# A two-stage attention kernel: scores and q@kv as row halves, fp32r turns of x, a power on GpSimd for the norms, and a written order of work

## The chip, the cores and the metric

The kernel runs on one core of a Trainium2 chip. A core has five engines with queues of their own: TensorE (PE; its weight loads are listed apart as PEld), VectorE (DVE), ScalarE (ACT), GpSimd (POOL) and SyncE (SP), which here only issues DMAs. Each takes its instructions in the order in which the program wrote them, and waits on semaphores. TensorE's products land in PSUM, eight banks of 512 fp32 values on 128 partitions; everything else lives in SBUF. The metric is the device time of one execution in microseconds (us), as a median over runs.

## The reference

Two layers in a row, on 8 batches of 576 tokens. The first is linear attention with 8 heads of 64 and an RMS norm for each head and token:

```python
kv = np.einsum('bhsd,bhse->bhde', k, v)
out = np.einsum('bhsd,bhde->bhse', q, kv)
rms = np.sqrt(np.mean(out * out, axis=-1, keepdims=True) + 1e-06)
x = out / rms * g_norm            # then heads side by side: 512 features
```

The second is a mixture of four causal attention experts with a head of 64; each token uses the two experts with the highest gate logits:

```python
logits = x @ w_gate               # top 2 of 4, softmax over the two
q, k, v = x @ wq[e], x @ wk[e], x @ wv[e]
a = softmax(causal(scale * (q @ k.T)))
out += w[e] * (a @ v @ wo[e])     # for the token's two experts
```

## The kernel before

Tokens are cut into five blocks, four of 128 and a last one of 64. The kernel writes its work as named tasks, one or a few instructions each: `("out", b, i)` is q@kv of block i in batch b. `graph` (line 48) lists all tasks with an engine, a cost and what they need; `plan` (line 270) puts them in one order: it follows the engines on a model of their time, and among the tasks that can start within 0.025 us on the engine that is free first it takes the one with the lowest `urgency` (line 257), a due time from a table per kind of task, batch and index. `SWAP` (line 28) says which PSUM copies go to the other one of ScalarE and VectorE. The order is written out under a manual schedule, so each engine's queue holds its share of that one list, and tasks of neighbouring batches are interleaved in it.

The stages of a batch, with their lines:

- Loads. k and v of a batch come in two DMAs each (four in batch 0) and a remainder for the last 64 tokens; q of batches 0 and 1 comes in token blocks of [tokens, 512] and is turned by TensorE transposes (`q`, line 625; copy `qc`); q of the others comes in eight DMAs, as 32-token pieces, and is turned by VectorE. In batch 0 half of the loads are issued on ScalarE's queue, and behind them the norm's and gate's weights (`lg0`, line 552, eight DMAs). Projection weights come as `lw` and are multiplied by g_norm (`ws`, line 582, four on GpSimd and two on VectorE).
- `kv` (line 599): k^T v of two heads at once, as column halves of 64: one head's result lies on PSUM partitions 0 to 63, the other's on 64 to 127. `kvx` (line 612) copies it into a block-diagonal matrix of two heads, with zeros elsewhere, `kvc` (line 618) copies it once more, compactly; `kt`, `ktc`, `kg`, `kgc` (lines 638 to 665) turn that, multiply it by the gate weights and put the products beside kv, so that q@kv gives gate logits with it.
- `out` (line 667): q@kv, for each block four fp32 products of 128 rows and 136 columns (two heads of 64 and 4). `oc` copies it to o_sb, `sq` squares it on ScalarE, `red` sums on VectorE.
- `nw` (line 699): the inverse square root of all five blocks at once, as a bit trick and three Newton steps in eleven small VectorE operations. `gl`, `lg`, `m8`, `sh`, `ex`, `mk`, `gt`, `den`, `rd`, `gate` make the gates from it, all on VectorE but the exponential. `xm` (line 747) multiplies o_sb by it on GpSimd into x_tok; `x` (line 758) turns x_tok by four fp32 transposes a block, and `xc` copies it to xT as fp32r.
- `v`, `qp`, `kp` (lines 808 to 835) are the projections, for two experts at once (p = 0, 1). `kpc` (line 841) copies k in two halves, one for each expert, into tiles whose other 64 rows stay zero.
- `sc` (line 853): scores of two experts and one piece of keys. Each product contracts 128 rows, of which the zeros of kT blot out the other expert's. Four pieces j hold 2, 4, 4 and 2 products, of 512; 64 and 448; 320 and 192; and 64 columns. `exp` on ScalarE, the causal cut `msk` on GpSimd.
- `pv`, `rc`, `iv`, `oc2` weigh v by the scores and scale by gate and sum; `ot`, `otc` turn it; `y` (line 945) multiplies by wo, `yc` copies, `st` stores.

PSUM is split into three tiles of two banks ("bg": out, projections, scores, pv) and two of one bank ("sm": the rest), taken in turn.

Of the kernel before, what the change touches and what calls it, by code (L numbers as in the profile page):

```python
# [10 lines left out]
FP32 = mybir.dt.float32  # L11
FP32R = mybir.dt.float32r
BF16 = mybir.dt.bfloat16
I32 = mybir.dt.int32
# [3 lines left out]
NB, NCH, EP = 5, 4, 2  # L18
QPE = 2
# [3 lines left out]

LOADS = ("lk", "lv", "lkr", "lvr", "lq", "lg0", "lw", "lwo", "st")

SWAP = {
    "ws": (('q', 0), ('v', 0),), "qc": ((0, 4), (1, 0), (1, 1), (1, 3),),
    "oc": ((0, 0), (0, 1), (1, 2), (1, 3), (1, 4), (6, 1), (6, 2), (6, 3), (7, 2), (7, 3),),  # L30
    "xc": ((0, 0), (0, 1), (1, 0), (1, 2), (1, 4), (6, 0), (6, 2), (6, 3), (7, 2), (7, 4),),
    "vc": ((0, 0), (6, 0), (6, 1), (6, 2),), "qpc": ((0, 0), (1, 0), (7, 0), (7, 1),),
    "kpc": ((0, 0), (6, 0), (7, 0),), "otc": ((0, 1), (1, 0), (1, 1), (6, 0), (6, 1),),
    "yc": ((0, 1), (0, 4), (1, 0), (1, 1), (1, 2), (1, 3), (1, 4), (6, 2), (6, 3),), "kvx": ((1,), (6,), (7,),),
    "kvc": ((1,),), "ktc": ((7,),),
}


def swapped(n):
    return n[1:] in SWAP.get(n[0], ())  # L40


def earlier(n, m):

    return len(n) > 1 and isinstance(n[1], int) and n[1] < m[1]


def graph(B):
    t = {}

    def add(name, eng, hold, lat, needs=(), tiles=()):
        t[name] = (eng, hold, lat, [n for n in needs if n in t], list(tiles))

    def pe(name, hold, needs, tiles=()):
        add(name, "PE", hold, hold + 0.27, needs, tiles)

    def act(name, took, needs, tiles=()):
        add(name, "ACT", took - 0.10, took + 0.06, needs, tiles)

    def dve(name, took, needs, tiles=()):  # L60
        add(name, "DVE", took - 0.05, took + 0.05, needs, tiles)

    def pool(name, took, needs, tiles=()):
        add(name, "POOL", took - 0.03, took + 0.10, needs, tiles)

    def copy(name, on_act, on_dve, needs, tiles=(), first=dve):

        ways = ((dve, on_dve), (act, on_act))
        if first is act:
            ways = ways[::-1]  # L70
        make, took = ways[swapped(name)]
        make(name, took, needs, tiles)

    R5, R4, R2 = range(NB), range(NCH), range(EP)
    for b in range(B):

        q2 = "ACT" if b == 0 else "SP"
        for p in R4 if b == 0 else R2:
            lat = 0.92 if b == 0 else 1.84
            add(("lk", b, p), "SP", 0.55, lat, (), (("k", b),))  # L80
            add(("lv", b, p), q2, 0.55, lat, (), (("v", b),))
        add(("lkr", b), "SP", 0.65, 0.67, [("kv", b - 2, c) for c in R4])
        add(("lvr", b), q2, 0.65, 0.67, [("kv", b - 2, c) for c in R4])
        for i in R5 if b < QPE else range(8):
            lat = (1.32 if i < NF else 0.66) if b < QPE else 1.06
            add(("lq", b, i), q2 if i % 2 else "SP", 0.6, lat, (), (("q", b),))
        if b == 0:
            add(("lg0",), "ACT", LG0, 0.3)
            dve(("wg",), 0.85, [("lg0",)])
            for nm in "qkv":  # L90
                for p in R2:
                    add(("lw", nm, p), "SP", 0.55, 0.92, (), (("x", nm, p),))
                    name, nd = ("ws", nm, p), [("lw", nm, p), ("lg0",)]
                    (dve if swapped(name) else pool)(name, 0.60 if swapped(name) else 1.08, nd, (("x", nm, p),))
# [912 lines left out]
```

The softmax here doesn't subtract the row's maximum and nothing guards it: scores larger than these inputs give would overflow.

## Time and profile before

| what | value |
|---|---|
| median of 3 runs (lowest to highest) | 252.12 us (252.02 to 252.76) |
| profiled execution: span from first to last instruction | 250.9 us |
| profiled execution: own time | not listed apart; the median lies 1.2 us above its span |
| busy: PE, PEld, DVE, ACT, POOL | 221.2, 199.0, 180.0, 148.8, 81.1 us |
| mean granted TensorE clock | 0.977 |

The profile page gives each engine's busy time, the span in 40 slices in tenths, the chain of work that ended last, and groups of instructions: line, engine, operation, output<-inputs, shape and count, then busy time in us and mean of one in ns, then the engine's idle time just before them with what ended it. A matmul's record lasts from its start to a modelled end, and records of a stream overlap; so a group's mean is no price, and the distance between records is.

### The profile page before, as it was taken

Reading aid. Unit: us, or ns where it says so; the run is one execution under the profiler, and the core shown is the slowest. Engines: PE = TensorE matmul, PEld = TensorE weight load, DVE = VectorE, ACT = ScalarE, POOL = GpSimd, SP = SyncE. Lnnn points to the kernel's source line nnn. Section 1 sums busy time; section 2 is a strip of 40 time slices with the busy share of each in tenths; the row PEclk is TensorE's granted clock in tenths of the full one; section 3 lists DMA queues with packets and bytes.
Section 4 is the critical chain, followed back from the end, with each engine's and each line's share of the span. In section 5 each row is a group of like instructions: output and inputs, shape, how many; then the busy total and the mean of one; then the engine's idle time right before and its main releaser. Section 6 shows DMA issues by size and latency. Waiting matters only on the chain.

```text
span 250.9 us, 6366 instructions
## 1 busy us (share of the span) xinstructions
PE 221.2 (88%) x2456; PEld 199.0 (79%) x2456; DVE 180.0 (72%) x510; ACT 148.8 (59%) x258; POOL 81.1 (32%) x159
## 2 busy tenths in 40 slices
PE   0726957999999999999999998989999699999982
PEld 0714847999999879996998988979988699888850
DVE  0084698688898978998699928976878887794560
ACT  0003450664923976359738993488899556838973
POOL 8300016604800256006700920066006600902310
PEclk9999995999999999999999999999999899999998
DMA  6997999999999989895999993021034100104245
GB/s 172 302 163 223 288 243 283 231 135 285 189 161 332 136 165 343 120 240 184 247 129 272 220 167 103 3 86 42 3 123 173 42 0 3 43 3 146 79 156 189
DMA packets 99433, 40.28 MB, mean 161 GB/s; under 512 B 76618, under 2 KB 94538, under 8 KB 99402
## 3 DMA queue, kind: packets, MB, share of 16 engines
q1 hardware_dynamic: 94320, 38.15, 65.8%
q10 hardware_dynamic: 5082, 1.72, 3.2%
q8 instruction: 19, 0.31, 0.6%
q14 instruction: 12, 0.10, 0.2%
HBM read 30.43 MB, written 9.44 MB: 159 GB/s over the span
## 4 chain that ended last, share of the span: by engine, by line
PE 71%; DVE 11%; DMA 7%; ACT 7%; issue 1%; SPq 1%; ACTq 0%; DVEq 0%
PE p_out L670 13%; PE p_sc L858 9%; PE p_v L811 8%; PE p_k L829 7%; PE p_q L829 7%; PE p_kv L607 6%; PE p_x L625 6%; PE p_y L948 6%; PE p_pv L892 6%; DMA q_b<-in_q_dram 3%; ACT PT L872 3%; DMA k_b<-in_k_dram 3%; DVE sh L776 2%; PE p_q L625 2%; PE p_ot L936 1%
## 5 line engine op out<-in xcount | busy, mean ns | idle before, releaser
L878 POOL TENSOR_SCALAR_AFFINE_SELECT PT<-PT 128x256 bf16<-128x256 bf16 (+1 forms) x80 | 29.0, 383 | 102.0 <-ACT PT L872 87.0
L751 POOL TENSOR_TENSOR x_tok<-o_sb,rs 128x512 f32<-128x512 f32 (+1 forms) x40 | 41.6, 1121 | 54.0 <-DVE rs L725 51.5
L872 ACT ACTIVATE PT<-p_sc 128x128 bf16<-128x128 f32 (+1 forms) x64 | 51.4, 849 | 6.9 <-PE p_sc L858 6.5
L670 PE MATMUL p_out<-kvx,qT 128*128 128x136 f32 x320 | 44.8, 290 | 0.7 <-DVE kvx L493 0.5
L670 PEld LDWEIGHTS p_out<-kvx,qT 128*128 128x128 f32 x320 | 41.9, 199 | 1.4 <-DVE kvx L493 0.5
L858 PE MATMUL p_sc<-qTp,kT 128*128 128x64 f32 (+4 forms) x192 | 39.8, 335 | 0.6 <-ACT PT L872 0.4
L690 ACT ACTIVATE sq<-o_sb 128x512 f32<-128x512 f32 (+1 forms) x40 | 25.3, 637 | 19.2 <-DVE o_sb L493 16.8
L858 PEld LDWEIGHTS p_sc<-qTp,kT 128*128 128x128 f32 x192 | 28.5, 190 | 4.4 <-ACT PT L872 1.1
L696 DVE TENSOR_REDUCE ms<-sq 128x8 f32<-128x520 f32 (+1 forms) x40 | 27.2, 682 | 5.8 <-ACT sq L690 5.5
L493 DVE COPY o_sb<-p_out 128x544 f32<-128x544 f32 (+1 forms) x30 | 21.6, 719 | 13.3 <-PE p_out L670 12.8
L607 PE MATMUL p_kv<-v_b,k_b 128*64 128x64 f32 x512 | 21.7, 236 | 7.6 <-DMA k_b<-in_k_dram 7.5
L811 PE MATMUL p_v<-wv_r,xT 128*128 128x256 f32 x160 | 26.6, 296 | 0.9 <-DVE vext L493 0.7
L625 PE MATMUL p_x<-ident_f,x_tok 128*128 128x128 f32 (+1 forms) x160 | 23.4, 279 | 3.9 <-DVE mk L785 2.2
L607 PEld LDWEIGHTS p_kv<-v_b,k_b 128*64 128x64 f32 x512 | 19.3, 148 | 9.4 <-DMA v_b<-in_v_dram 7.3
L948 PE MATMUL p_y<-wo_b,OT 128*128 128x512 bf16 x80 | 22.7, 381 | 1.0 <-ACT xT L491 0.7
L811 PEld LDWEIGHTS p_v<-wv_r,xT 128*128 128x128 f32 x160 | 21.6, 189 | 2.2 <-DVE vext L493 1.0
L625 PEld LDWEIGHTS p_x<-ident_f,x_tok 128*128 128x128 f32 (+1 forms) x160 | 17.9, 146 | 6.2 <-issue 3.2
L491 ACT CAST xT<-p_x 128x512 fp32r<-128x512 f32 (+1 forms) x30 | 15.7, 546 | 10.6 <-PE p_x L625 10.5
L829 PE MATMUL p_k<-xT,wk_r 128*128 128x288 f32 x128 | 20.2, 301 | 0.0
L491 ACT COPY y<-p_y 128x512 f32<-128x512 f32 (+1 forms) x31 | 17.8, 593 | 3.8 <-PE p_y L948 2.6
L829 PE MATMUL p_q<-xT,wq_r 128*128 128x288 f32 x128 | 19.1, 299 | 0.0
L491 ACT CAST kT<-p_k 64x576 fp32r<-64x576 f32 x26 | 16.5, 634 | 4.2 <-PE p_k L829 4.0
(89 smaller groups left out, 325.1 us busy)
## 6 DMA issues: line engine op xcount, KB each, us to landing
out_dram<-y SPq DMA_DIRECT2D x32, 256.0 KB, 2.2
k_b<-in_k_dram SPq DMA_DIRECT2D x14, 512.0 KB, 5.5
v_b<-in_v_dram SPq DMA_DIRECT2D x14, 512.0 KB, 7.1
q_b<-in_q_dram SPq DMA_DIRECT2D x48, 144.0 KB, 4.8
q_b<-in_q_dram SPq DMA_DIRECT2D x6, 256.0 KB, 8.2
k_rem<-in_k_dram SPq DMA_DIRECT2D x8, 128.0 KB, 3.9
v_b<-in_v_dram ACTq DMA_DIRECT2D x4, 256.0 KB, 6.5
k_b<-in_k_dram SPq DMA_DIRECT2D x4, 256.0 KB, 6.3
```

Source lines behind the costliest of these rows:

```text
L491: nc.scalar.copy(dst, src)
L607: nc.tensor.matmul(p_kv[hh * Dh : (hh + 1) * Dh, c, :], lhsT=lhs, rhs=rhs, start=(j == 0), stop=(j == NF), skip_group_check=True,)
L625: nc.tensor.transpose(p_t[:, c, :nt], chunk(c)[:nt], ident_f[:nt, :nt])
L670: nc.tensor.matmul(p_o[:, c // 2, (c % 2) * 256 : (c % 2) * 256 + 2 * GW], lhsT=blocks_of(qT, c)[:, i * P : (i + 1) * P], rhs=kvx[b % 2][: ...
L696: nc.vector.tensor_reduce(mss[b % 2][:nt, i, :], sqs[(NB * b + i) % 3][:nt], axis=AX_X, op=AluOpType.add)
L751: nc.gpsimd.tensor_tensor(out=buf(("x", b, i), [P, NCH, P], FP32, "x_tok")[:nt].rearrange("p c (h r) -> p h r c", h=H), in0=ob[:nt, i, :, ...
L811: nc.tensor.matmul(p_v[:], lhsT=blocks_of(xTs[b % 2], c)[:, i * P : (i + 1) * P], rhs=w_r["v"][:, c, :, :].rearrange("p e f -> p (e f)"), ...
L829: nc.tensor.matmul(p_p[:, s, 0:HALF], lhsT=w_r[nm][:, c, 2 * pr : 2 * pr + 2, :].rearrange("p e f -> p (e f)"), rhs=blocks_of(xTs[b % 2], ...
L858: nc.tensor.matmul(p_s[:, el, o : o + hi - lo], lhsT=kTs[pr][el][:, kb * P : (kb + 1) * P], rhs=tiles["qTp", b, pr][:, lo:hi], start=True, ...
L872: nc.scalar.activation(PT[:, :, d0 : d0 + o], big("sc", b, pr, j)[:, :, 0:o], ACTF.Exp, scale=scale)
L878: nc.gpsimd.affine_select(out=d, in_=d, compare_op=AluOpType.is_ge, fill=0.0, base=0, pattern=[[0, 2], [1, w]], channel_multiplier=-1,)
L948: nc.tensor.matmul(p_y[:], lhsT=blocks_of(OTs[b % 2], pr)[:, qc * P : (qc + 1) * P], rhs=wo_b[:, pr, :], start=(pr == 0), stop=(pr == EP - 1),
```

## The change

Each part in the words of the code:

- **Scores.** kT is one tile of 128 rows with both experts' keys (three of them in turn), copied by one instruction. A product takes one expert's 64 rows of kT and of qT; the two experts' products go to different PSUM banks.
- **q@kv.** kvx is compact: for each pair of heads, the heads' kv side by side with their gate columns at the outer ends. A block takes eight products of 64 rows and 68 columns, alternating between the lower and the upper 64 rows, into two banks. The copies `kvx` and `kvc` become one, and `kt` reads kvx.
- **Head pairs.** Heads c and c + 4 are always paired, in all batches; so q of batches 0 and 1 is loaded in two DMAs for each block (it was one), and the gate weights for the other pairing go (two DMAs fewer in `lg0`).
- **Gates of kv (`kg`).** Four products with an output of 64 columns of the array each, two for each half, in place of two full ones; one copy.
- **Norms.** The mean's factor 1/64 goes into g_norm (`g8` multiplies by 8). `pw` raises a block's sums to the power -0.5 on GpSimd, one operation of 128x8 for each block; Newton is gone. 18 of 40 squares are done on GpSimd by a multiplication. Of the small gate operations, 7 of 8 `sh`, 3 of 8 each of `gl`, `gt` and `gate`, and 19 of 32 `iv` are on GpSimd.
- **x.** Its turn is an fp32r product with an identity, in all blocks with 128 rows.
- **Last y block.** 64 tokens by 512 columns become two column halves, on partitions 0 to 63 and 64 to 127; the copy is 128x256, the store two DMAs.
- **Order, engines and buffers.** `graph`, `plan` and the tables go. The order of all tasks, the engine of each, and the slot of each buffer stand in three strings; PSUM is four pairs of banks, in which a task takes a pair or one bank as the string says. Moved with it: 25 of 40 o_sb copies on ScalarE (10 before), 14 of 40 xT copies (30 before), 20 of 40 vext copies (4 before), all weight products on VectorE.

```diff
-    kTs = []
-    for pr in range(EP):
-        pair = []
-        for el in range(2):
-            t = const.tile([P, NB, P], FP32R, name=f"kT{pr}{el}")
...
     def k_proj_copy(b, pr):
-        for el in range(2):
-            pb = slice(el * Hd, (el + 1) * Hd)
-            copy(
-                ("kpc", b, pr), kTs[pr][el][pb, 0:S].rearrange("p (s n) -> p s n", s=2), big("k", b, pr)[pb, :, 0:HALF]
-            )
+        t = kTs[(2 * b + pr) % 3]
+        copy(("kpc", b, pr), t[:, 0:S].rearrange("p (s n) -> p s n", s=2), big("k", b, pr)[:, :, 0:HALF])
...
         for kb, lo, hi in PIECES[j]:
             for el in range(2):
+                pp = slice(el * Hd, (el + 1) * Hd)
                 nc.tensor.matmul(
                     p_s[:, el, o : o + hi - lo],
-                    lhsT=kTs[pr][el][:, kb * P : (kb + 1) * P],
-                    rhs=tiles["qTp", b, pr][:, lo:hi],
+                    lhsT=kTs[(2 * b + pr) % 3][pp, kb * P : (kb + 1) * P],
+                    rhs=tiles["qTp", b, pr][pp, lo:hi],
...
-    def kvx_copy(b):
-        p_kv = small(None, "kv", b)[:, 0]
-        for hh in range(2):
-            pp = slice(hh * Dh, (hh + 1) * Dh)
-            copy(("kvx", b), kvx[b % 2][pp, :, hh, 0:Dh], p_kv[pp, :, :])
+    def kv_copy(b):
+        copy(
+            ("kvc", b), kvx[b % 2][:, :, E : E + 2 * Dh],
+            small("kv", b)[:, 0 : NCH * Dh].rearrange("p (m f) -> p m f", m=EP),
+        )
...
         for c in range(NCH):
-            nc.tensor.matmul(
-                p_o[:, c // 2, (c % 2) * 256 : (c % 2) * 256 + 2 * GW],
-                lhsT=blocks_of(qT, c)[:, i * P : (i + 1) * P],
-                rhs=kvx[b % 2][:, c, :, :].rearrange("p a g -> p (a g)"),
+            for hh in range(2):
+                pp = slice(hh * Dh, (hh + 1) * Dh)
+                nc.tensor.matmul(
+                    p_o[:, hh, c * GW : (c + 1) * GW],
+                    lhsT=blocks_of(qTs[b % NQT], c)[pp, i * P : (i + 1) * P],
+                    rhs=kvx[b % 2][pp, c // 2, c % 2 * GW : (c % 2 + 1) * GW],
...
+    def pw(b, i):
+        nc.gpsimd.tensor_tensor(
+            out=rstds[b % 2][:, i * H : (i + 1) * H], in0=mss[b % 2][:, i, :],
+            in1=minus_half[:].to_broadcast([P, H]), op=AluOpType.pow,
+        )
...
     def x_tr(b, i):
-        transpose_in(i, lambda c: tiles["x", b, i][:, c, :], "x", b, i)
+        p_t, nt = small("x", b, i), blocks[i][1]
+        for c in range(NCH):
+            nc.tensor.matmul(
+                p_t[:, c * P : c * P + nt], lhsT=tiles["x", b, i][:, c, :], rhs=ident_r[:, 0:nt], start=True, stop=True
+            )
...
     def sh(b):
-        nc.vector.tensor_tensor(
+        ew(("sh", b)).tensor_tensor(
...
     def y_mm(b, qc):
-        p_y = small([P, D], "y", b, qc)
+        p_y, (s0, nq) = small("y", b, qc), blocks[qc]
         for pr in range(EP):
-            nc.tensor.matmul(
-                p_y[:], lhsT=blocks_of(OTs[b % 2], pr)[:, qc * P : (qc + 1) * P], rhs=wo_b[:, pr, :],
-                start=(pr == 0), stop=(pr == EP - 1),
-            )
+            lhs = OTs[b % 2][:, pr * S + s0 : pr * S + s0 + nq]
+            for o in range(P // nq):
+                w = D * nq // P
+                nc.tensor.matmul(
+                    p_y[o * nq : (o + 1) * nq, 0:w], lhsT=lhs, rhs=wo_b[:, pr, o * w : (o + 1) * w],
+                    start=(pr == 0), stop=(pr == EP - 1), skip_group_check=True,
+                )
...
+    psum = ctx.enter_context(tc.tile_pool(name="ps", bufs=1, space=bass.MemoryType.PSUM))
+    pairs = [psum.tile([P, 2, 512], FP32, name=f"p_{j}") for j in range(4)]
+    def small(*key):
+        n = place(("sm",) + key)
+        return pairs[n // 2][:, n % 2, :]
...
     with tc.manual_schedule():
-        for t, _, n in plan(tasks, POOLS, {n: urgency(n) for n in tasks})[0]:
+        for n in order:
             emit[n[0]](*n[1:])
```

## The prediction

> **What bounds the kernel now.** I read the page's span, busy times and slices first, then the busy time by stage, the groups of instructions, and last the chain of waits, for prices.
>
> ```profile
> span 250.9 us, 6366 instructions
> ...
> PE 221.2 (88%) x2456; PEld 199.0 (79%) x2456; DVE 180.0 (72%) x510; ACT 148.8 (59%) x258; POOL 81.1 (32%) x159
> ...
> PE   0726957999999999999999998989999699999982
> ...
> PEclk9999995999999999999999999999999899999998
> ```
>
> The reader sees TensorE full from the seventh slice to the end. By stage (columns: PE, PEld, DVE, ACT, POOL, clock, DMA share, GB/s):
>
> ```profile
> 0.00:60.00 60.00, 40.65 (x436) 36.79 (x438) 35.25 (x93) 17.29 (x32) 16.84 (x45) 0.94 1.00 227
> 60.00:150.00 90.00, 89.13 (x1080) 82.09 (x1077) 74.47 (x217) 61.19 (x107) 34.29 (x59) 1.00 1.03 212
> 150.00:240.00 90.00, 85.92 (x899) 77.51 (x898) 67.35 (x190) 64.87 (x109) 29.59 (x55) 0.98 0.19 63
> 240.00:251.00 11.00, 5.46 (x54) 2.58 (x51) 2.96 (x12) 5.49 (x11) 0.41 (x1) 0.93 0.50 180
> ```
>
> TensorE idles 19.4 us in the first 60, 0.9 in the next 90, 4.1 in the third stage and 5.5 at the tail: 29.8 us of 250.9. Only TensorE work, the start and those gaps can pay. The costliest TensorE groups:
>
> ```profile
> L670 PE MATMUL p_out<-kvx,qT 128*128 128x136 f32 x320 | 44.8, 290 | 0.7 <-DVE kvx L493 0.5
> ...
> L858 PE MATMUL p_sc<-qTp,kT 128*128 128x64 f32 (+4 forms) x192 | 39.8, 335 | 0.6 <-ACT PT L872 0.4
> ```
>
> Their busy times hold pipeline tails, so prices come from pieces of the chain of waits (start, us, what):
>
> ```profile
> 55.51 1.31 PE p_kv L607 x40
> ...
> 101.42 0.47 PE p_v L811 x4
> ...
> 109.41 2.48 PE p_kv L607 x80
> 111.89 0.68 PE p_v L811 x4
> ...
> 121.19 0.93 PE p_out L670 x8
> ...
> 234.80 0.47 PE p_sc L858 x2
> ...
> 236.15 1.37 PE p_sc L858 x10
> ```
>
> A q@kv block costs 0.93 us: eight records (each fp32 product shows as two), 0.116 apart. One head pair's twelve score products cost 0.47 + 1.37 = 1.84. The kv records are 2.48/80 = 0.031 apart: the two column halves run side by side. The price of a weight load and the worst stall, from the timeline:
>
> ```profile
> 25.16 0.52 PEld L651 LDWEIGHTS p_kg<-wg_bd,kvT 128*128 128x128 f32 x4 [0.61 <-issue]
> ...
> 193.06 3.93 DVE L776 TENSOR_TENSOR sh<-lg,m 128x20 f32<-128x20 f32 x1
> ```
>
> Four 128-column loads, each about 0.19 long, fit in 0.52, so they follow one another by (0.52 - 0.19)/3 = 0.11 us. This decides what row halves are worth.
>
> **What the skill says.** "TensorEngine Tiling (Array Packing)", section Tiling Modes: tiles load and multiply in parallel, but a change of mode drains the array. The trace agrees for column halves; of two row halves at once it shows nothing. "TensorE: Matmul & The Clock Gate", section LDWEIGHTS: load time goes by columns, not rows. The 64-column kv loads agree (half of 0.11 is 0.055, and a pair takes 0.062 side by side); a 64-row load of a plain product isn't in the trace. "GPSIMD Engine Reference", section Performance versus the Vector engine: GpSimd takes about twice VectorE's time for two inputs; x_tok's 1.12 us for 512 elements against VectorE's 0.68 for the weights' 512 is 1.6 times. No page prices its power.
>
> **The change on TensorE, step by step.**
>
> Scores: each product takes its head's 64 rows in place of 128 rows, half of them zeros; a pair should run at once. Pair times from the pieces, scaled by columns with 0.11 as floor: 512 columns 0.235; 448, 0.20; 320, 0.145; 192, 0.11; 64 twice, 0.11 each. Sum 0.91 against 1.84: -0.93 x 16 = -14.9.
>
> q@kv: eight products of 68 columns in place of four of 136. Sixteen records in eight pairs: a stream would take 0.058 but the load 0.11, so 8 x 0.11 = 0.88 for 0.93: -0.05 x 40 = -2.0. Bounds: 8 x 0.058 = 0.47 if half-row loads are quicker or hidden (-18.4); 16 x 0.11 = 1.76 if the halves' loads take turns (+33). I take the middle: kv's halves load side by side.
>
> Gates as column halves: four 0.11 loads become four pairs of 0.062: -0.2 x 8 = -1.5. Last y block: 0.43 to 0.22: -1.7. x as fp32r products: load-bound at 0.11, where a transpose now takes 0.11 (0.44 a block), so nothing; the last block goes from 64 rows to a full tile: the group's busy time is 3.7/8 = 0.46 for it against 19.8/32 = 0.62 for a full one: +0.16 x 8 = +1.3.
>
> Changes of mode: in the two written orders TensorE changes between full tiles, row halves and column halves 39 times before and 147 times after. Entering kv costs 0.14 (1.31 for 40 records, 1.17 for 40 more), leaving it 0.21 (v 0.68 for 0.47); other exits are about 0.11. At 0.13 each, 108 x 0.13 = +14.0 (0.11 to 0.18: +12 to +19).
>
> TensorE's sum: -14.9 - 2.0 - 1.5 - 1.7 + 1.3 + 14.0 = -4.8.
>
> **The other engines.** Removed from VectorE: Newton's 88 small operations (17.5 us), kvx copies (4.1), most of sh (7), about 19 of the gate products iv (4), half the o_sb copies (11), constant kT fills (3.9); added: xT copies and weight products (about 14); less some vext copies (7): 180 to some 140. ScalarE loses half of kT's copies (two of 0.63 become one of 0.65: about 9) and 18 squares (11), and gains o_sb and vext copies (15): about 140. GpSimd gains 18 squares at x_tok's 1.12 (20), 40 powers and some 35 small operations (9), and loses four weight products (4). A power on 128x8 is between the 0.10 of an 8-element memset and the 1.12 of x_tok; I take 0.3, so 12 us: 118 in all. All three lie beside TensorE's 216; without that cover 40 powers are the 12 (4 to 45). DMA: q of two batches in twice the issues, last stores too: some 18 issues of 0.6 on SP and ACT. SP's run ahead under TensorE; ACT's first issues stay 15, since two gate loads go (its q issues in halves against 1.2 us less). kvc is behind them on ACT, at 20.0 now, and kt, gates and q@kv wait for kvc: no gain is counted there.
>
> **Start.** Now all five reductions must end (34.1) before eleven Newton steps of 0.2, and the first x_tok starts at 36.9. Then each block has its own power and can go on alone; kvx before kvc is gone, and projection weights are loaded earlier. But loads at 227 GB/s bring the weights and first two batches' 9 MB only by some 40 us, so of 19.4 idle I count -5 (0 to -10). The clock at 0.94 over 60 us is 3.6 us lost to half speed around 38 to 45, after the idle stretch; with steadier work -3. The stall at 193 was VectorE's sh while GpSimd ran x_tok; seven of eight sh move to GpSimd, which queues them in turn: of 4.1 idle and 1.8 of clock in that stage -4 (0 to -5). Tail: the last copy is 256 columns of 128 rows in place of 512 of 64: -0.3; the 2.4 us to land stays. Late next: the TensorE queue itself.
>
> **Sum.** 250.9 - 4.8 - 5 - 3 - 4 - 0.3 = 233.8 of span; the median of the runs is 1.2 us above the profiled span (the execution has no separate time shown), so **235.0**.
>
> **Rivals.** (1) Half-row loads are hidden: q@kv at 0.47 (another -16.4) and the narrow score pairs near 0.06 (-2.5): about 216. For: kv's 0.062 pairs. Against: 128 columns to load, not 64. (2) Slower: row halves' loads take turns: q@kv at 1.76 gives +35 against my sum, scores 0.22+0.44+0.44+0.22 = 1.32 for 0.91 +7: 277. It decides from a block of about 0.93 + 17/40 = 1.36 us. For: no row pair in the trace; against: kv. The power belongs on this side only past some 3 us each, when GpSimd's 106 + 120 would become the bound. (3) Mode changes eat it: at 0.25 each 13 us more, with start and stalls unchanged where others take their place: 248 to 255. For: exits of 0.21; against: exits of 0.11.
>
> **How the numbers follow.** A measurement tells 0.3% (0.8 us) from no change. My case 0.58, its own range 225 to 246; rival 1 0.18; rival 2, with a dear power, 0.14; rival 3 0.10, of it 0.06 faster, 0.03 same, 0.01 slower. Faster 0.58 + 0.18 + 0.06 = 0.82, same 0.03, slower 0.15. The range takes in rival 1 and the lower part of rival 3, 213 to 253, and leaves out rival 2 and some ends.
>
> **What would show it.** p_sc's twelve products in about 0.9 us; p_out's sixteen records in 0.88 (0.47 or 1.76 the rivals); the piece after a q@kv or score run longer by 0.1 to 0.2; PE busy near 216; first x before 33 us; no half clock near 40; powers near 0.3 us. I am wrong if row pairs don't overlap, a power takes microseconds, or TensorE stays as busy and only waits elsewhere.

## The result, and the profile after

| | time, us | ratio to before [95%] |
|---|---|---|
| before, beside it on the same chip | 252.44 (252.02 to 254.51) | 1 |
| changed kernel | 324.84 (323.52 to 326.75) | 1.2834 [1.2747, 1.2921] |

The forecast was 235.0, its range 213 to 253. The changed kernel is 28% slower. The page of its profiled execution:

```profile
span 321.4 us, 7019 instructions
...
PE 261.1 (81%) x2824; PEld 221.3 (69%) x2824; DVE 141.1 (44%) x354; ACT 134.8 (42%) x233; POOL 165.8 (52%) x244
...
PE   0257956999979689967999789997899699969982
...
PEclk9999999995999855996599856996599959986998
```

VectorE and ScalarE came out as forecast (141.1 for some 140, 134.8 for some 140). GpSimd is at 165.8 where 118 was expected. The PE row has dents all along, where before it was full from the seventh slice on; and below the dents the clock row now falls to half, again and again. By stage (PE, PEld, DVE, ACT, POOL, clock, DMA share, GB/s):

```profile
0.00:60.00 60.00, 34.00 (x251) 29.87 (x252) 15.96 (x41) 11.44 (x22) 20.67 (x43) 1.00 0.74 179
60.00:150.00 90.00, 78.75 (x989) 68.43 (x989) 41.28 (x105) 39.93 (x71) 57.92 (x68) 0.85 0.69 143
150.00:240.00 90.00, 81.05 (x873) 70.07 (x875) 45.59 (x111) 39.48 (x68) 45.23 (x67) 0.77 0.62 132
240.00:322.00 82.00, 67.35 (x719) 52.95 (x715) 38.22 (x100) 43.90 (x73) 42.02 (x68) 0.89 0.17 59
```

The clock was 1.00 and 0.98 in the two middle stages before; it is 0.85 and 0.77 now. (The 1.00 of the first stage isn't a grant, as is shown below.) The costliest groups, among them the operation that had no row before:

```profile
L444 POOL TENSOR_TENSOR rstd<-ms,minus_half 128x8 f32<-128x8 f32 x40 | 65.6, 1646 | 14.0 <-DVE ms L441 12.0
...
L477 PE MATMUL p<-ident_r,x_tok 128*128 128x128 f32 (+1 forms) x160 | 34.6, 354 | 25.1 <-POOL x_tok L466 20.1
...
L416 PE MATMUL p<-kvx,qT 64*128 64x68 f32 x640 | 45.3, 297 | 1.5 <-DVE kvx L259 0.9
```

A power of 128x8 elements takes 1.646 us on GpSimd. The forecast took 0.3 and held 1.12 for the upper bound. TensorE's turns of x wait for x_tok 20.1 us, where that wait was hardly there before. The list of TensorE's waits names the same releaser, and besides it little but the start (the next entry is 3.1 us) (columns: us in total, times, longest):

```profile
PE p L477 <- POOL x_tok L466: 20.1, 15, 2.5
PE p L401 <- DMA q_b<-in_q_dram: 13.7, 2, 13.5
```

One such stall in the timeline (start, us, what; in brackets the idle time before and what ended it):

```profile
102.69 3.24 POOL L444 TENSOR_TENSOR rstd<-ms,minus_half 128x8 f32<-128x8 f32 x2
...
105.89 1.04 POOL L437 TENSOR_TENSOR sq<-o_sb 128x512 f32<-128x512 f32 x1
...
106.88 1.63 POOL L444 TENSOR_TENSOR rstd<-ms,minus_half 128x8 f32<-128x8 f32 x1
...
108.48 1.07 POOL L466 TENSOR_TENSOR x_tok<-o_sb,rstd 128x512 fp32r<-128x512 f32 x1
...
109.60 0.74 PE L477 MATMUL p<-ident_r,x_tok 128*128 128x128 f32 x4 [2.45 <-POOL x_tok L466]
```

GpSimd has three powers and a square to do before this x_tok; TensorE has idled 2.45 us when it arrives, and its queue is in order, so nothing behind passes it. After the 3.4 us window that starts at 106.6, in which this stall lies, the clock goes to half.

One thing in the clock rows misleads. None of these traces has a clock record ahead of the first grant of full clock, and the page counts that time as full. The first grant comes at 24.2 us before and at 58.8 us in the changed kernel. Ahead of it the weight loads show half clock. Two pieces of the changed kernel's timeline, loads of q@kv ahead of the first grant and in a stretch recorded at full clock:

```profile
29.89 1.78 PEld L416 LDWEIGHTS p<-kvx,qT 64*128 64x128 f32 x16 [0.98 <-DVE kvx L259]
...
99.83 1.87 PEld L416 LDWEIGHTS p<-kvx,qT 64*128 64x128 f32 x32
```

Sixteen loads took about as long as thirty-two at full clock. The loads of x from 42 to 53 us are 0.213 us apart as well, against 0.11 at full clock; so TensorE ran the first 58.8 us at half. Before, four loads of q took 0.72 us at 22.3 us, ahead of the first grant, and 0.42 at 33.5. The mean clocks of the pages (0.977 before, 0.868 now) are too high by this.

From the trace's records of products and of the clock, the span can be taken apart without remainder: TensorE's idle time before and between products; its busy time restated at full clock (busy time less half of what falls in half-clock stretches, the time ahead of the first grant among them); the other half of that, lost to the clock; and what follows the last product. In us, for the profiled executions of before, after, and the experiments below:

| kernel | idle | work at full clock | lost to half clock | after the last product | span |
|---|---|---|---|---|---|
| before | 25.4 | 211.8 | 9.4 | 4.3 | 250.9 |
| after | 55.2 | 206.6 | 54.5 | 5.0 | 321.4 |
| e1, no power | 38.4 | 209.1 | 26.2 | 5.1 | 278.8 |
| e3, before with scores as halves | 25.4 | 209.1 | 8.8 | 4.3 | 247.6 |
| e4, before with q@kv as halves | 24.9 | 214.9 | 29.3 | 4.3 | 273.4 |
| e5, e4 with wide streams | 27.4 | 219.4 | 9.7 | 4.3 | 260.9 |
| e6, before with fp32r turns of x | 26.5 | 212.8 | 11.3 | 4.3 | 254.8 |
| e7, e1 with wide streams and transposes | 40.3 | 209.8 | 10.3 | 5.1 | 265.4 |
| e8, after with wide streams and transposes | 59.6 | 207.5 | 33.4 | 5.0 | 305.5 |

Of the 70.5 us that the span grew, 29.8 are idle time, 45.1 are lost to the clock, 0.8 the tail, and the work fell by 5.2. (e7 and e9 below issue the same products and show 209.8 and 209.7 us of work; the changed kernel and e1 do too, and show 206.6 and 209.1, so the restated work is good to some 3 us.) The profiled executions of e1, e4 and e8 were the slowest of their four runs, up to 2% above the median of these, and the ratios leave such slow executions out.

### The profile page after: what moved, and what is told of

Its sections match the earlier page's. It is cut to its first block, busy times and chain, and to the rows that moved or that the text cites. A ratio compares the mean times of both kernels' runs of the same rounds, so it can differ in the third digit from the quotient of the medians.

```text
span 321.4 us, 7019 instructions
## 1 busy us (share of the span) xinstructions
PE 261.1 (81%) x2824; PEld 221.3 (69%) x2824; DVE 141.1 (44%) x354; ACT 134.8 (42%) x233; POOL 165.8 (52%) x244
## 4 chain that ended last, share of the span: by engine, by line
PE 31%; POOL 10%; DVE 3%; issue 3%; ACT 2%; DMA 1%; DVEq 0%; POOLq 0%; ACTq 0%
PE p L551 6%; POOL rstd L444 5%; PE p L416 5%; PE p L532 4%; PE p L578 4%; PE p L477 3%; PE p L670 3%; PE p L612 3%; POOL x_tok L466 3%; POOL sq L437 2%; PE p L363 1%; PE p L655 1%; DMA out_dram<-y 1%; DVE osc L640 1%; DVE y L259 1%
## 5 line engine op out<-in xcount | busy, mean ns | idle before, releaser
L444 POOL TENSOR_TENSOR rstd<-ms,minus_half 128x8 f32<-128x8 f32 x40 | 65.6, 1646 | 14.0 <-DVE ms L441 12.0
L592 ACT ACTIVATE PT<-p 128x1024 bf16<-128x1024 f32 (+1 forms) x64 | 51.1, 841 | 22.0 <-PE p L578 20.7
L477 PE MATMUL p<-ident_r,x_tok 128*128 128x128 f32 (+1 forms) x160 | 34.6, 354 | 25.1 <-POOL x_tok L466 20.1
L477 PEld LDWEIGHTS p<-ident_r,x_tok 128*128 128x128 f32 x160 | 29.9, 262 | 33.4 <-POOL x_tok L466 26.2
L416 PE MATMUL p<-kvx,qT 64*128 64x68 f32 x640 | 45.3, 297 | 1.5 <-DVE kvx L259 0.9
L416 PEld LDWEIGHTS p<-kvx,qT 64*128 64x128 f32 x640 | 42.4, 208 | 4.1 <-DVE kvx L259 1.0
L466 POOL TENSOR_TENSOR x_tok<-o_sb,rstd 128x512 fp32r<-128x512 f32 x40 | 43.3, 1096 | 1.3
L532 PE MATMUL p<-wv_r,xT 128*128 128x256 f32 x160 | 38.2, 381 | 0.3 <-ACT xT L257 0.2
L532 PEld LDWEIGHTS p<-wv_r,xT 128*128 128x128 f32 x160 | 31.0, 266 | 3.9 <-issue 1.7
L578 PE MATMUL p<-qTp,kT 64*128 64x64 f32 (+4 forms) x192 | 28.8, 398 | 1.1 <-ACT PT L592 0.7
```

The lines of the kernel that those rows point to most:

```text
L416: nc.tensor.matmul(p_o[:, hh, c * GW : (c + 1) * GW], lhsT=blocks_of(qTs[b % NQT], c)[pp, i * P : (i + 1) * P], rhs=kvx[b % 2][pp, c // 2, ...
L444: nc.gpsimd.tensor_tensor(out=rstds[b % 2][:, i * H : (i + 1) * H], in0=mss[b % 2][:, i, :], in1=minus_half[:].to_broadcast([P, H]), op=Al ...
L466: nc.gpsimd.tensor_tensor(out=buf(("x", b, i), [P, NCH, P], FP32R, "x_tok")[:].rearrange("p c (m k r) -> p m k r c", m=NCH, k=2), in0=ob[: ...
L477: nc.tensor.matmul(p_t[:, c * P : c * P + nt], lhsT=tiles["x", b, i][:, c, :], rhs=ident_r[:, 0:nt], start=True, stop=True)
L532: nc.tensor.matmul(p_v[:, 0 : E * Hd], lhsT=blocks_of(xTs[b % 2], c)[:, i * P : (i + 1) * P], rhs=w_r["v"][:, c, :, :].rearrange("p e f -> ...
L578: nc.tensor.matmul(p_s[:, el, o : o + hi - lo], lhsT=kTs[(2 * b + pr) % 3][pp, kb * P : (kb + 1) * P], rhs=tiles["qTp", b, pr][pp, lo:hi], ...
```

## The experiments

Two theories stood at first. **The power**: at 1.65 us it sits between a block's sum and its x_tok, and TensorE waits. **The row halves**: they cost more than forecast, in loads that take turns or in changes of mode. A third came out of the first four runs, **the clock**: it is granted not by how busy TensorE is but by how much of the array's rows is streaming, so products that are bound by their weight loads keep it at half. In e1, e7 and e9 a multiplication by 0.1 stands in the power's place, so the norm is left out there.

### e1: the changed kernel without the power

```diff
-    nc.gpsimd.memset(minus_half[:], -0.5)
+    nc.gpsimd.memset(minus_half[:], 0.1)
...
-            in1=minus_half[:].to_broadcast([P, H]), op=AluOpType.pow,
+            in1=minus_half[:].to_broadcast([P, H]), op=AluOpType.mult,
```

> The changed kernel with the power replaced by a multiplication of the same 128x8 operands by 0.1 at the same places (the norm is left out, x is scaled by its own mean square instead; all other work stays). Power theory: the 40 powers of 1.65 us on GpSimd hold x_tok back, TensorE waits for it (26 us) and then runs at half clock after each wait (about 35 us lost); without them 250 to 270 us, half clock rare. Rival, the row halves and the 147 changes of array mode cost TensorE far more than 0.13 us each: 295 us or more, with TensorE as busy as now.

Measured: 280.4 us, ratio 1.0999 [1.0906, 1.1092]: above the 250 to 270 of the power theory, below the rival's 295, and half clock isn't rare (60.6 us recorded). The operation's group in the full list of groups:

```profile
L444 POOL TENSOR_TENSOR rstd<-ms,minus_half 128x8 f32<-128x8 f32 x40 | 8.3, 212 | 26.9 <-DVE ms L441 21.9 <-DVE g_den L517 3.2 <-DVE inv L633 1.7
```

The same instruction with another operator takes 0.212 us in place of 1.646; 40 times that difference is 57.4 us of GpSimd, and 44 us of the time goes with it (324.84 - 280.4), though GpSimd is busy only half of the span. TensorE's wait for x_tok falls from 20.1 us to 0.9. So the power is the largest single cause; but without it the kernel is still 10% slower than before.

### e2: the power on ScalarE, as logarithm and exponential

```diff
-        nc.gpsimd.tensor_tensor(
-            out=rstds[b % 2][:, i * H : (i + 1) * H], in0=mss[b % 2][:, i, :],
-            in1=minus_half[:].to_broadcast([P, H]), op=AluOpType.pow,
-        )
+        r = rstds[b % 2][:, i * H : (i + 1) * H]
+        nc.scalar.activation(r, mss[b % 2][:, i, :], ACTF.Ln)
+        nc.scalar.activation(r, r, ACTF.Exp, scale=-0.5)
```

> The changed kernel with the power on ScalarE as Ln and then Exp of -0.5 times it (nothing left out). Power theory: 80 small ScalarE operations of about 0.22 us (18 us on an engine that is 42% busy) in place of 66 us on GpSimd: as the multiplication or up to 10 us slower, 250 to 280 us; if Ln and Exp lie in different tables each pair costs two table loads of about 1.3 us, over 100 us on ScalarE, and the time is above 300. Rival (TensorE's modes): 295 or more in any case.

Measured: 388.75 us, ratio 1.5271 [1.5161, 1.5382]; slower than the power itself. A group of its page:

```profile
L446 ACT ACT_TABLE_LOAD x40 | 51.3, 1283 | 0.7
```

A second such row stands for line 445: 80 table loads, 102.6 us, of ScalarE's 249.2, since logarithm and exponential follow each other in turn, and in this program each change from one to the other loads a table. "ScalarE activation tables: per-element evaluation and per-set limits" in the Trainium skill, section What a function is on this engine, says that two functions in different sets are one load of 1283 ns apart; the trace agrees to the ns. x_tok then waited 98.6 us for ScalarE's rstd. The run doesn't clear the power, it only puts a longer wait in its place: what counts is how late rstd is, on whatever engine.

### e3 and e4: before, with one of the two row-half parts alone

e3, scores (and the single kT tile for each head pair):

```diff
-                    lhsT=kTs[pr][el][:, kb * P : (kb + 1) * P],
-                    rhs=tiles["qTp", b, pr][:, lo:hi],
+                    lhsT=kTs[pr][pp, kb * P : (kb + 1) * P],
+                    rhs=tiles["qTp", b, pr][pp, lo:hi],
```

> The kernel before with the scores alone as row halves (one kT tile per expert pair, k still copied in two halves, same order). My prices: twelve products 0.91 us in place of 1.84, -14.9 us; changes of mode 113 in place of 39, 74 x 0.13 = +9.6; 243 to 252 us, likeliest 247. Rival (row halves are the loss): above 257.

Measured: 250.93 us, ratio 0.9868 [0.9832, 0.9904]. The score group of its page:

```profile
L852 PE MATMUL p_sc<-qTp,kT 64*128 64x64 f32 (+4 forms) x192 | 25.3, 350 | 0.8 <-ACT PT L866 0.5
```

Its busy time fell from 39.8 to 25.3 us, by 14.5; the forecast had 14.9. The changes of mode, 39 before and 113 here, take a good part of it back (74 at the forecast's 0.13 are 9.6), and the restated work falls by 2.7 only. So this part of the change is a gain by itself, and both kernels are slower than it.

e4, q@kv:

```diff
-                lhsT=blocks_of(qT, c)[:, i * P : (i + 1) * P],
-                rhs=kvx[b % 2][:, c, :, :].rearrange("p a g -> p (a g)"),
+                    lhsT=blocks_of(qT, c)[pp, i * P : (i + 1) * P],
+                    rhs=kvx[b % 2][pp, c, hh, :],
```

> The kernel before with q@kv alone as row halves (eight products of 68 columns; kvx stays block-diagonal, same order). My prices: 0.88 us a block in place of 0.93, -2.0 us; changes of mode 91 in place of 39, 52 x 0.13 = +6.8; 254 to 261 us, likeliest 257. If half-row loads were quicker: below 245; if they took turns: above 280.

Measured: 270.11 us, ratio 1.0616 [1.0541, 1.0691]: far above my 254 to 261, and below the 280 of loads that take turns. The records show that the halves do run side by side: the two of a pair mostly start 6 to 15 ns apart (3 to 7 in e3's scores), and pairs follow each other by 0.112 us at full clock, as forecast. Restated at full clock the work is 214.9 us, against 211.8. What it lost most is the clock: 60.7 us of recorded half-clock stretches in its profiled execution (275.25 us) for 13.7 before, and no more idle time than before. TensorE is busy 244.2 us, 89% of the span (before: 221.2), and yet gets half the clock. That doesn't fit a clock that follows busy time, and it began the third theory.

### e5: e4 with wider streams

The second half of each row-half product's columns is thrown away: the next product overwrites it, and the last one stays narrow. Instructions, weight loads, waits and changes of mode stay as they were; only the streams are twice as long.

```diff
+                n = 2 * c + hh
+                w = GW if n == 7 else 2 * GW
                 nc.tensor.matmul(
-                    p_o[:, hh, c * GW : (c + 1) * GW],
+                    p_o[:, hh, c * GW : c * GW + w],
...
-                    rhs=kvx[b % 2][pp, c, hh, :],
+                    rhs=kvx[b % 2][pp].rearrange("p c a g -> p (c a g)")[:, n * GW : n * GW + w],
```

> The run of the kernel before with q@kv as row halves, with each product's stream widened from 68 to 136 columns (the second 68 are overwritten by the next product, so nothing is left out; one of eight stays at 68). Same instructions, loads, changes of mode and waits; a pair is load-bound at 0.11 us either way. New theory, the clock follows the share of the array that streams (rows x columns over a 3.4 us window: below about 0.4 it is halved, and it comes back only above about 0.75 of the halved clock): the share of q@kv rises from 0.6 to 1.0 and, at half clock, from 0.53 to 1.0, so half clock falls from 61 us to under 25, and the time from 270 to 254 to 260 us. Rival, the loss lies in the changes of mode or in waits of the row halves: 267 us or more, as before the widening.

Measured: 263.44 us, ratio 1.0227 [1.012, 1.0335]. Giving TensorE more to do made the kernel faster, from 1.0616 to 1.0227. The clock rows of e4 and of e5:

```profile
PEclk9977575557999999999999999999999757979999
```

```profile
PEclk9965597799999999999999999999999999999999
```

e4's second half-clock stretch is gone and the first is shorter; the loss to half clock falls from 29.3 to 9.7 us, and the recorded half clock from 60.7 to 26.4 (forecast: under 25). The time stayed some 3 us above the range forecast for it, which leaves room for the 52 further changes of mode (forecast: 6.8 us).

### e6: before, with fp32r turns of x alone

```diff
-        transpose_in(i, lambda c: tiles["x", b, i][:, c, :], "x", b, i)
+        for c in range(NCH):
+            nc.tensor.matmul(
+                p_t[:, c, :nt], lhsT=tiles["x", b, i][:nt, c, :], rhs=ident_r[:nt, :nt], start=True, stop=True
+            )
```

> The kernel before with x turned by fp32r products alone (same order). At full clock a product is 0.111 us where the transpose was 0.109, so by the price list +0.3 us in all, 252 to 256. By the clock theory the share of x's blocks falls from 1.0 to 0.48, and the half clock after the first idle stretch, in which x runs, is left later: half clock 20 to 35 us in place of 14, 256 to 264 us.

Measured: 258.48 us, ratio 1.0138 [1.0048, 1.0228]: a small loss, inside the clock theory's 256 to 264. Its half clock isn't what that theory forecast, though: 17.5 us are recorded, not 20 to 35, and 1.9 us more than before are lost to the clock; so the run doesn't show where its loss lies. An fp32r product of 128 columns streams half as long as the fp32 transpose, but it follows the one before at the same distance, 0.11 us, since the weight load sets it.

### e7 and e8: wide streams and transposes, without and with the power

e8 is the changed kernel with q@kv's streams widened as in e5 and x by transposes as before; e7 is e1 with the same edits.

```diff
+                w = GW if c == 3 else 2 * GW
...
-                    p_o[:, hh, c * GW : (c + 1) * GW],
+                    p_o[:, hh, c * GW : c * GW + w],
...
-                p_t[:, c * P : c * P + nt], lhsT=tiles["x", b, i][:, c, :], rhs=ident_r[:, 0:nt], start=True, stop=True
-            )
+            nc.tensor.transpose(p_t[:, c * P : c * P + nt], tiles["x", b, i][:nt, c, :], ident_f[:nt, :nt])
```

> The changed kernel with the multiplication in place of the power (as in the first run: the norm is left out), q@kv's streams widened to 136 columns (six of eight) and x turned by fp32 transposes again. Clock theory: half clock from 61 us to under 30, time from 280 to 250 to 265 us. Rival, the written order starves TensorE and the clock only follows its waits: 275 us or more.

> The changed kernel, power kept, with q@kv widened and x by transposes (nothing left out). The waits for the power still halve the clock each batch, but it should come back after one or two windows of 3.4 us in place of four or five: half clock from 87 to 35 to 60 us, time from 325 to 290 to 310 us. Rival (the clock isn't held down by small shares): 318 us or more.

Measured: e7 270.14 us, ratio 1.0536 [1.044, 1.0633], above its range of 250 to 265; e8 302.13 us, ratio 1.1816 [1.1733, 1.1898], within its own, with 64.6 us of recorded half clock, above the 35 to 60 forecast. With e1 and the changed kernel this makes a square. In hundredths of the time before: the changed kernel is 28.3 above it, without the power 10.0, without the thin streams 18.2, without both 5.4. The power is worth 18.3 where streams are thin and 12.8 where they are wide; the streams 10.2 with the power and 4.6 without. ("Thin" streams are those of the changed kernel, bound by their weight loads: q@kv's of 68 columns and x's fp32r products.) The two feed each other: a wait for x_tok takes the clock down, and thin streams keep it down. e8 shows this: it idles no less than the changed kernel (59.6 and 55.2 us) and has as many recorded half-clock stretches (nine and eight), but loses 25.8 us to them and not 38.1; and it has its first grant of full clock at 35.1 us and not at 58.8.

### e9: where e7's start goes

TensorE's first product starts at 13.7 us in e7 and at 6.8 before, for a q block waits at the head of its queue. Here that block (and its copy) stands behind two kv halves. The order, decoded from the string:

```diff
-    order: ... lq 0 3, q 0 1, lk 0 2, kv 0 1, qc 0 1, lq 0 4, g8, lq 0 2, wg, kv 0 0, ...
+    order: ... lq 0 3, lk 0 2, kv 0 1, lq 0 4, g8, lq 0 2, wg, kv 0 0, q 0 1, qc 0 1, ...
```

> The kernel of e7 (the changed kernel with a multiplication by 0.1 in the power's place, so the norm is left out, with widened q@kv streams and x by transposes), with one edit: q block 1 of the first batch and its copy stand behind two kv column halves in the written order, where they stood ahead of them. Theory 1 (that block's late load at the head of TensorE's queue costs the start): first TensorE work at 7 to 9 us in place of 13.7, and 264 to 268 us in place of 270. Theory 2 (the loads as a whole, 9 MB at the measured rate, set when the first q@kv can begin): TensorE starts earlier but the first q@kv stays near 30 us, and the time stays within 1 us of 270.

Measured: 269.33 us beside 254.04 for before, ratio 1.065 [1.0578, 1.0721]; e7 had 270.14 (the two ratios' intervals overlap). TensorE starts at 8.4 us; it waits for a load until then, and for another after its first products:

```profile
PE p L363 <- DMA v_b<-in_v_dram: 8.4, 1, 8.4
PE p L363 <- DMA v_rem<-in_v_dram: 4.1, 1, 4.1
```

The first q@kv starts at 28.9 us (e7: 28.5; before: 26.2). So the order of the head of the queue is not the cause, and start and time came out as the second theory said. Its reason, the loads as a whole, isn't shown: from 20 to 30 us the DMA engines are busy for 0.54 of the time in e9 and for 1.00 before, and in the first 60 us SyncE's queue, which issues loads, stands 9.7 us in waits that TensorE's turns of x end and 5.7 in one that its turns of q end. So loads are held back in their turn, and what sets the start stays open.

### e10: a version faster than both

Before with the scores as row halves and one k copy of 128 rows in place of two of 64, its cost in `graph` lowered to match.

```diff
-            copy(("kpc", b, p), 1.24, 1.50, [("kp", b, p)] + [("sc", b - 1, p, j) for j in R4], (("bg", "k", b, p),), act)
+            copy(("kpc", b, p), 0.65, 0.76, [("kp", b, p)] + [("sc", b - 1, p, j) for j in R4], (("bg", "k", b, p),), act)
...
-        for el in range(2):
-            pb = slice(el * Hd, (el + 1) * Hd)
-            copy(
-                ("kpc", b, pr), kTs[pr][el][pb, 0:S].rearrange("p (s n) -> p s n", s=2), big("k", b, pr)[pb, :, 0:HALF]
-            )
+        copy(("kpc", b, pr), kTs[pr][:, 0:S].rearrange("p (s n) -> p s n", s=2), big("k", b, pr)[:, :, 0:HALF])
```

> The kernel before with the scores alone as row halves (e3) and, besides, one copy of k's projection over 128 rows in place of two over 64, with the planner's costs for it set to 0.65 and 0.76 us; the planned order moves with them. Theory 1 (TensorE's queue sets the time; the copies lie beside it): 249 to 253 us, ratio 0.98 to 1.00, as e3. Theory 2 (VectorE's and ScalarE's copies hold up the k products): 245 to 249. A slower order from the planner would show as over 255.

Measured: 248.99 us beside 254.04, ratio 0.9828 [0.9784, 0.9872]. It is faster than before by 1.7%, and than the changed kernel by 23%. Its time lies on the border between the two expectations, and its interval overlaps e3's, so whether the saved copies are worth anything beyond the scores isn't settled.

### e11 and e12: the clock by itself

Everything of the reference is left out in both; TensorE runs products one after the other without a wait. "TensorE: Matmul & The Clock Gate" in the Trainium skill, section What's actually happening, says that the clock is granted by how busy TensorE has recently been, in windows of about 3.4 us. The windows agree with every trace here (half-clock stretches of 3.4, 6.8, 10.2, 13.7, 17.1 us); e4 had raised doubts about the measure.

```python
SEGMENTS = (
    (128, 128, 96), (64, 128, 128), (64, 64, 96), (64, 128, 96), (128, 128, 64), (64, 96, 96), (128, 128, 64),
    (64, 112, 128), (32, 128, 96), (128, 96, 64), (128, 32, 96), (128, 80, 64), (128, 128, 48),
)
...
nc.tensor.matmul(banks[n % 4][0:cols, :], lhsT=q_h[0:rows, 0:cols], rhs=q_h[0:rows, :], start=True, stop=True)
```

> Everything of the reference is left out; it measures the clock by itself. TensorE runs bf16 products of 512 columns back to back, without a wait between them, in thirteen stretches with different tiles (rows x columns x count): 128x128x96, 64x128x128, 64x64x96, 64x128x96, 128x128x64, 64x96x96, 128x128x64, 64x112x128, 32x128x96, 128x96x64, 128x32x96, 128x80x64, 128x128x48. Theory 1 (the granted clock follows the share of the array that streams: it falls to half below about 0.40, and comes back from about 0.75 of the halved clock): full in the 2nd (share 0.50), half in the 3rd (0.25) and still in the 4th (0.50), full in the 5th, half in the 6th (0.375), full in the 7th and 8th (0.44), half in the 9th (0.25), back to full in the 10th (0.75), half in the 11th (0.25) and still in the 12th (0.625), full in the last: some 380 us in all. Theory 2 (the clock follows TensorE's busy time alone): after the first few us full in every stretch, some 255 us of products, as TensorE is never idle.

Stretches 2 (64 rows), 3 (64 rows, 64 columns), 9 (32 rows) and 11 (128 rows, 32 columns) in a table by window; columns: PE, PEld, DVE, POOL, clock, DMA share, GB/s:

```profile
27.00:54.00 27.00, 27.00 (x126) 11.66 (x124) 0.00 (x0) 0.00 (x0) 1.00 0.00 1
54.00:75.00 21.00, 21.00 (x98) 10.28 (x98) 0.00 (x0) 0.00 (x0) 1.00 0.00 0
...
172.00:211.00 39.00, 39.00 (x98) 13.36 (x96) 0.00 (x0) 0.00 (x0) 0.53 0.00 0
...
227.00:248.00 21.00, 21.00 (x98) 9.27 (x98) 0.00 (x0) 0.00 (x0) 1.00 0.00 1
```

Neither theory as written holds. TensorE is busy in every us of all four, so busy time is not the measure: 32 rows get half the clock. But columns don't count: 64x64 and 128x32, each a quarter of the array, stay at full clock, where the share of the whole array had promised half. What counts is the share of rows. (In the kernels the two readings nearly agree: their products of 64 columns are column halves of 128 rows, two side by side, and below such a pair is counted as one stream.)

e12 asks for the rest with the kernel's own forms, and with the same form before and after a fall to half clock.

```python
SEGMENTS = (
    ("full", 96), ("x_r", 160), ("rows32", 64), ("x_r", 160), ("full", 64), ("half68", 160), ("rows32", 64),
    ("half68", 160), ("half136", 160), ("rows32", 64), ("rows64", 96), ("x_t", 160), ("full", 48),
)
...
elif kind == "x_r":
    nc.tensor.matmul(o[:, 0:P], lhsT=q_r[:, c], rhs=ident_r[:], start=True, stop=True)
...
        banks[2 * (n % 4) + hh][:, 0:w], lhsT=q_b[pp, c], rhs=q_b[pp, 0:w], start=True, stop=True
```

> Everything of the reference is left out; as in e11, TensorE runs one stretch after the other without a wait, now with this kernel's forms: full (bf16, 128 rows, 512 columns, x96), x_r (fp32r products of 128 columns, as the changed kernel turns x, x160), rows32 (bf16, 32 rows, 512 columns, x64), x_r x160 again, full x64, half68 (pairs of fp32 row-half products of 68 columns, as the changed q@kv, x160), rows32 x64, half68 x160 again, half136 (the same pairs with 136 columns, x160), rows32 x64, rows64 (bf16, 64 rows, x96), x_t (fp32 transposes of 128 columns, x160), full x48. e11 showed that columns do not count (64x64, 64x96 and 128x32 stayed at full clock) and 32 rows do. Theory 1 (the granted clock follows the share of rows times the share of cycles in which they stream, with two borders: below about 0.40 it falls to half, and from half it comes back only at about 0.75 of the halved clock): half in every rows32; after it still half in the second x_r (0.48; about 0.21 us each), in the second half68 (0.53; about 0.21 a pair) and in rows64 (0.50; 0.43 each), which stay full in their first stretch (0.11, 0.11) or did so in e11 (0.22); back to full in half136 and in x_t. Theory 2 (rows alone count, however short the stream): x_r and half68 go back to full within 7 us of their second beginning, rows64 too if 64 rows suffice, and half136 begins at full. Theory 3 (one border without memory): each form has the same clock in both of its stretches.

The same table; in order x_r, x_r again, half68, half68 again, half136, rows64, x_t:

```profile
27.00:45.00 18.00, 18.00 (x163) 17.90 (x162) 0.00 (x0) 0.00 (x0) 1.00 0.00 1
...
68.00:102.00 34.00, 34.00 (x161) 34.00 (x160) 0.00 (x0) 0.00 (x0) 0.50 0.00 1
...
117.00:153.00 36.00, 36.00 (x642) 35.86 (x642) 0.00 (x0) 0.00 (x0) 1.00 0.01 2
...
178.00:246.00 68.00, 68.00 (x639) 67.92 (x638) 0.00 (x0) 0.00 (x0) 0.50 0.00 1
247.00:285.00 38.00, 38.00 (x626) 38.00 (x626) 0.00 (x0) 0.00 (x0) 0.95 0.01 2
...
308.00:348.00 40.00, 40.00 (x95) 13.67 (x93) 0.00 (x0) 0.00 (x0) 0.50 0.00 0
349.00:368.00 19.00, 19.00 (x157) 19.00 (x156) 0.00 (x0) 0.00 (x0) 0.89 0.00 1
```

The first theory holds in every stretch, and the other two fall. The same 160 turns of x take 18 us after full streams and 34 after a fall; the same 640 records of q@kv 36 us and then 68, all of it at half, without a gap. Widened to 136 columns the same pairs are back at full clock 4.5 us later, and so are fp32 transposes after some 5 us. 64 rows in bf16 keep a full clock (e11) and never win it back (here, 40 us at half). So there are two borders. From the windows of before, after, e1 and e8, with the share as (columns x cycles for a column x rows / 128) over the window's cycles (2.4 a ns or half of it; a column takes one in bf16 and fp32r, 512 of them 0.217 us in e11, and two for each record in fp32): of the windows at full clock all up to 0.34 are followed by half, those of 0.34 to 0.38 go either way, none above 0.38 is; of those at half clock most return from 0.75 on, and the highest that didn't had 0.77, the lowest that did 0.58. The windows ahead of the first grant fit: the last of them had 0.75 to 1.02 in the four kernels, and none ahead of it more than 0.69.

## Why the prediction was wrong

Term by term, forecast against the table of the span:

- **TensorE's own work, -4.8.** This part held. Row halves run side by side; q@kv's pairs are 0.112 us apart (0.11); the scores' products lost 14.5 us (14.9); x costs its load. The restated work is 206.6 for 211.8, which is -5.2 (e1: 209.1, -2.7), good to some 3 us.
- **The power, 0.3 us "beside TensorE's 216".** The step that failed first, twice over. The size: 1.646, above the bound that I drew from x_tok's 1.12. That bound rested on element counts, and a power isn't bound by elements: it has 8 for each partition, the multiplication in its place took 0.212, so my 0.3 was the price of an ordinary operation of that shape. The place: I compared GpSimd's busy sum with TensorE's and found cover. But rstd stands between the sum and x_tok of each block, behind the other blocks' powers in one queue, and TensorE's queue waits for x_tok in order. For the same reason the limit in rival 2, "only past some 3 us each", was wrong: 1.65 us with GpSimd busy half the time cost 44 us (e1). Waits for x_tok, 20.1 us, are the largest part of the 29.8 that idle time grew; I had counted idle time as falling.
- **The clock, -3 "with steadier work" and part of -4 for stalls.** It is +45.1, the largest term, and the step had the wrong sign. I took half clock for a thing that follows idle time only, as the half-clock stretches on record before did, and I overlooked that the start runs at half: 4.9 us are lost ahead of the first grant before, and 16.4 in the changed kernel. Waits for x_tok take it down more often; and the changed q@kv and x, which stream half as long in the same load-bound distance, can't bring it back (e5, e8, e12). That q@kv and x came out at the same distance as before, which I booked as costing nothing, was the loss: with wide streams and transposes in e8 the first grant comes at 35.1 us in place of 58.8, and the clock loses 33.4 us in place of 54.5.
- **The start, -5.** TensorE is busy 34.0 us of the first 60 where it was 40.65, so idle time there is about +7, and nearly all of TensorE's work there runs at half clock. That loads bound all of it, as my 40 us for weights and q had it, doesn't fit: the DMA engines' share in these 60 us is 0.74, where it was 1.00. What sets the start isn't shown (e9).
- **Tail, -0.3:** +0.8.
- **Rivals.** Rival 2 had the sign, and 277 was nearer than 235, but its mechanism (loads that take turns) is false by e4 and e12. Rival 1 (hidden loads) is false by the same distances. Rival 3's dear changes of mode: a rough estimate from the restated work is 0.06 us each in e4 (3.1 us at 52 changes) and 0.16 in e3 (14.5 less 2.7 at 74), around the 0.13 that was used and below 0.25.

What stays open: e7, without the power and with wide streams, is still 5.4% above before, and the table puts all of it in idle time (40.3 for 25.4). About 6 us lie in the first 60 (34.3 busy for 40.65) and 6 in the next 90 (83.0 for 89.1), in many waits of about 1 us for copies, none of them a cause by itself. The written order of work, with its engines and buffers, is the main thing left that differs there, but no run undid it; that it is the cause isn't shown.

## What to carry to other kernels

Ask of an operation that replaces a chain not whether its engine has time, but who waits for its result, and price it by its own operator, not its shape. A product that is bound by its weight load and is made to stream less doesn't stay free: here it left the clock at half after each stall. So when a trace shows half clock under a busy TensorE, compare rows times streaming cycles before and after; and before a trace's first clock record, read the clock from the distance of weight loads. Try the parts of a large change alone: one of these gains 1.3%, and the rest hid it.

## What the runs showed of the hardware that was not expected

- GpSimd's power on 128x8 fp32 took 1.646 us; the same instruction with a multiplication 0.212.
- Alternating logarithm and exponential on ScalarE cost a table load of 1.283 us each time (80 loads, 102.6 us in e2).
- The granted clock follows rows times streaming cycles and has a memory: 64 rows without a gap kept full clock for 27 us (e11) and, after a fall, stayed at half for 40 (e12); 32 rows fell to half while TensorE never idled; 64x64 and 128x32 stayed at full clock, so the number of columns made no difference there.
- TensorE started at half clock, and could stay there long: the changed kernel had its first full clock at 58.8 us, 45 us after its first product.
- More streaming made a kernel faster: widening q@kv's products from 68 to 136 columns, with half of the result thrown away, took the ratio from 1.0616 to 1.0227.
